# A fused attention and mixture-of-adapters kernel: quads of x copied whole in batches 0 to 6, and another order table

## The chip, the cores and the metric

One core of a Trainium2 chip runs the whole kernel in one launch. The metric is the device time of one execution in microseconds (us). TensorE (PE) does matrix products and transposes into PSUM, eight banks of 512 fp32 columns. VectorE (DVE) and ScalarE (ACT) carry PSUM to SBUF and do the element-wise work. GpSimd (POOL) issues the loads, SyncE (SP) and ScalarE's queue the stores, and 16 DMA engines move the data.

## What is computed

Squared-ReLU attention over 8 batches, 12 heads, 448 positions and head size 64, and then, on its output as 3584 rows of 768, a top-2 mixture of 8 rank-16 adapters that is added to the row:

```
scores = q @ k.T / sqrt(64)
attn   = maximum(scores, 0)**2 / 448
x      = (attn @ v), heads joined: 3584 x 768
logits = x @ w_gate                      # 3584 x 8
w      = softmax over the two largest logits of a row
out    = x + sum over those two e of  w_e * (x @ A[e]) @ B[e]
```

## The kernel before

**Units of work.** The twelve heads of a batch are worked on in three *quads* of four; 24 quads in all, numbered batch by batch. A quad in batches 0 to 6 has seven *steps* (a block of 64 keys of each of the four heads), so steps 0 to 146; batch 7 is cut in two unequal parts of the rows and has steps 147 to 173. A *tile* is 128 rows of x: 28 tiles, in groups of three, the last alone. Every piece of work is an `Op` with a name and a number:

- `tp` transposes q or k of a quad on PE into PSUM (line 313), `te` copies the result to SBUF on DVE (`qT`, lines 327 and 335).
- `qk` n is the scores of step n on PE (line 452), `relu` n the ReLU of its 128x896 into `a` on ACT or DVE (lines 472 and 474), `sq` the square of two or three steps at once on DVE (line 489), `pv` n the product with v on PE (line 520).
- `x` copies the finished quad from PSUM to `xt`, as bf16, on ACT or DVE (line 565, function `xt_copy`). A quad stands in two banks, 448 columns in each, and is copied by two ops, one for each bank; in batch 7 there are four for a quad, of 322 and 126 columns.
- `z` is a tile's x times `awg`, which holds the eight adapters' A and the gate's weights side by side (128 columns of A, then 8 of the gate; line 582, 6 matmuls); `gmax`, `gd`, `gu`, `gt`, `gsg`, `gw`, `gzp` find the two largest logits and weigh z (lines 603 to 626), `zt` transposes it (line 644), `zT` copies it out (line 661).
- `b` is half a tile of the output: three matmuls that put x itself into the bank (line 728) and the product with B (line 737, two matmul instructions in fp32). In tiles 15 to 23 x comes instead by a transposing DMA on SP (`xb`, line 677), and `b` is the product with B alone. `o` moves the half tile to `osb` (ACT or DVE, line 773; in tiles 15 to 23 an addition on DVE, line 764), and `st` stores a tile of 384 KB (line 783) through SP, in tiles 24 and 26 through ACT's queue; tile 27 goes as two halves, SP and ACT.
- Ops without a name of their own are `f` and a number: f0 to f10 are the start, f11 to f83 the loads of 224 KB for a quad (two DMAs each, line 185) with the small weights, f84 to f91 the transposes and copies of quad 0. f24 loads B (line 248), f58 is q of quad 16, f80 is k of quad 23, f87 transposes the last four key blocks of quad 0 (`k_rest`).

**What sets the order.** Nothing is planned at run time or by the compiler: the string `ORDER` lists every op; `ordered()` walks it, and `kernel` calls each op's function in that order, which makes the order on every engine's own queue. A suffix `@n` gives the first PSUM bank of an op, `:A` or `:D` the engine of an evacuation. The durations in the `op(...)` calls, `take` and `give` and `lat` are for the search that made the table and reach no instruction. SBUF buffers come from pools (`POOLS`: five for q, five for k, eight for v, eleven for `a`, four for `osb`); a load or an evacuation whose pool is full waits on its queue until the earlier user of a buffer is done, and everything behind it on that queue waits as well.

PE works either in four 64x64 quadrants (`tp`, `qk`, `pv`) or with the whole array of 128x128 (`z`, `zt`, `b`, `aw`).

Of the kernel before, what the change touches and what calls it, by code (L numbers as in the profile page):

```python
# [33 lines left out]
C = dict(late=6, xi=(), om=(), merge_x=0, sqp=((999, (2, 2, 3)),), om2=(), fl=(), gf=(), ai=4, tg=((15, 3), (18, 3), (21, 3)), sp=(), xbdur=1.45, bx=8, xh=2, apart=3, apcap=1, gl=(3, 1), tqlat=2.0)  # L34
# [5 lines left out]
f4 f3 f1 f0 f2 f6 f5 f8 f7 f11 f9 f10 f84@0 f12 f88 f85@2 f90 f89 f13 f87@4 qk0@6 f91 qk1@0 relu0:D qk2@2 f14  # L40
relu1:A qk3@4 relu2:D relu3:A tp2@6 f17 qk4@0 te2 relu4:A qk5@2 qk6@4 sq2 tp3@6 f16 relu5:A f86@0 te3 relu6:A
sq0 qk7@0 f15 qk8@2 qk9@6 relu7:A tp4@4 relu8:D relu9:A f18 qk10@0 te4 qk11@2 relu10:A qk12@6 sq4 tp5@4 f19
relu11:A qk13@0 relu12:A te5 tp6@2 f26 sq9 relu13:A qk14@4 qk15@6 tp7 relu14:A f23 sq7 pv0@0 pv1 pv2 relu15:A
pv3 qk16@4 te6 pv4 pv5 f20 relu16:A pv6 qk17@6 x13:D pv7@2 relu17:A qk18@4 sq11 f22 pv8 pv9 x12:A qk19@6
relu18:A pv10 qk20@0 relu19:D f21 pv11 relu20:A pv12 pv13 qk21@4 sq16 x27:A qk22@6 f27 qk23@0 relu21:A aw1@3
sq14 relu22:A f33 x26:D relu23:A qk24@4 tp8@6 ae1 f25 relu24:A sq18 qk25@0 qk26@2 tp9 relu25:A f55 pv14@4 pv15
pv16 te8 relu26:A pv17 qk27@0 f31 pv18 pv19 relu27:A pv20 sq23 qk28@2 qk29@6 x41:A f28 qk30@0 x40:D relu28:A
aw0@5 sq25 relu29:A f29 relu30:A qk31@2 ae0 tp10@6 tp11 f32 relu31:A sq21 qk32@4 qk33@0 relu32:A te10 pv21@2 f30
pv22 pv23 relu33:A qk34@4 sq30 qk35@6 relu34:A qk36@0 f37 relu35:D relu36:A qk37@4 pv24 pv25 relu37:A pv26 sq32
f35 qk38@6 tp12@0 pv27 relu38:A tp13 qk39@4 f43 x55:A te12 qk40@6 x54:A z0@3 relu39:A sq35 qk41@0 f34 z1  # L50
relu40:A qk42@4 relu41:D z2 relu42:A f38 qk43@6 gmax0 tp14@0 relu43:A sq28 qk44@4 tp15 f42 relu44:A gd0 qk45@6
gu0 te14 relu45:A qk46@4 f50 gt0 sq39 qk47@0 relu46:A pv28@6 pv29 pv30 gsg0 pv31 f24 relu47:A qk48@4 pv32 gw0
pv33 sq44 f48 pv34 relu48:A qk49@0 gzp0 x69:A f36 tp18@4 sq37 relu49:A tp19 pv35@2 zt0@7 zt1 zt2 x68:A f41 te18
qk50@0 zT0:A pv36 pv37 relu50:A qk51@6 sq46 pv38 pv39 f47 relu51:A pv40 qk52@4 qk53@0 pv41 relu52:A x82:D tp16@6
tp17 relu53:A te16 qk54@4 b2@2 relu54:A f44 sq49 qk55@0 o2:A qk56@6 qk57@4 relu55:A relu56:D b0@2 f49 x83:A
relu57:D qk58@0 o0:A qk59@6 f39 relu58:A z3@3 z4 sq51 relu59:A qk60@4 qk61@0 z5 f40 sq56 relu60:A b4@2 relu61:A
gmax3 qk62@6 f46 sq58 b1@4 relu62:A gu3 gd3 qk63@0 o4:A gt3 f65 sq42 qk64@6 gsg3 o1:A b3@5 relu63:A gw3 gzp3
b5@2 f51 relu64:A sq60 zt3@4 zt4 o3:A zt5 pv42@0 o5:A pv43 st2 qk65@6 zT3:A sq53 pv44 pv45 relu65:A qk66@2 st4
pv46 pv47 pv48 relu66:A tp20@4 st0 qk67@6 x96:D tp21 x97:A te20 f53 pv49@2 relu67:A pv50 qk68@0 pv51 pv52 sq63
relu68:A pv53 f66 pv54 pv55 qk69@4 qk70@6 x110:A relu69:D qk71@0 relu70:A f45 b6@2 x111:D relu71:A qk72@4 o6:D  # L60
tp22@6 relu72:A sq65 qk73@0 tp23 pv56@2 relu73:A pv57 f74 qk74@4 te22 pv58 pv59 relu74:A pv60 qk75@0 f79 pv61
sq67 pv62 relu75:A qk76@6 b8@4 f64 relu76:A x124:D qk77@0 x125:A sq70 tp24@6 relu77:A tp25 qk78@2 f59 z6@5 te24
relu78:A qk79@0 z7 relu79:A f52 o8:D qk80@2 qk81@6 sq72 z8 relu80:A b10@4 f54 gmax6 relu81:A sq77 qk82@0 tp26@2
# [81 lines left out]
def build(k=None, c=C):  # L145
# [159 lines left out]
    def tp(b, q):  # L305
# [57 lines left out]
        if b >= c["bx"]:  # L363
            return turn_qk(b, q)
# [590 lines left out]
```

## Time and profile before

| what | value |
|---|---|
| median of three runs | 181.69 us (181.57 to 182.73) |
| span of the profiled execution, first to last instruction | 179.6 us |
| time of the profiled execution itself | not listed apart; median less span is 2.09 us |
| PE, DVE, ACT busy | 165.1, 163.5, 156.2 us |
| POOL busy | 90.7 us |
| granted clock of TensorE | 1.00 all through |

A row of the timeline gives the start of a run of equal instructions, the time from its start to the end of its last one, engine, line, operation, output and inputs, count, and in brackets the idle time of the engine ahead of it and what ended it. Instructions overlap at their ends, so the *pitch* of an operation (from its start to the start of what follows it on the engine without idle time) is shorter than its duration. The chain of waits lists start, length and owner of each piece of the work that ended last.

### The profile page before, as it was taken

Reading aid. Unit: us, or ns where it says so; the run is one execution under the profiler, and the core shown is the slowest. Engines: PE = TensorE matmul, PEld = TensorE weight load, DVE = VectorE, ACT = ScalarE, POOL = GpSimd, SP = SyncE. Lnnn points to the kernel's source line nnn. Section 1 sums busy time; section 2 is a strip of 40 time slices with the busy share of each in tenths; the row PEclk is TensorE's granted clock in tenths of the full one; section 3 lists DMA queues with packets and bytes.
Section 4 is the critical chain, followed back from the end, with each engine's and each line's share of the span. In section 5 each row is a group of like instructions: output and inputs, shape, how many; then the busy total and the mean of one; then the engine's idle time right before and its main releaser. Section 6 shows DMA issues by size and latency. Waiting matters only on the chain.

```text
span 179.6 us, 7694 instructions
## 1 busy us (share of the span) xinstructions
PE 165.1 (92%) x3366; PEld 99.2 (55%) x3366; DVE 163.5 (91%) x254; ACT 156.2 (87%) x240; POOL 90.7 (50%) x155
## 2 busy tenths in 40 slices
PE   7887998888899999999979899999999999999990
PEld 2445476454535665646646465655666557576650
DVE  0699999999989999999999899999999999999831
ACT  3399999999999999999998999999999899993120
POOL 7999997988869377850966867250000000000000
PEclk9999999999999999999999999999999999999999
DMA  4999999999999999994699999988495663515644
GB/s 90 126 170 188 164 112 183 164 180 178 202 180 152 186 303 166 175 166 130 84 176 299 197 185 268 237 118 222 113 171 149 45 223 63 189 42 211 230 194 158
DMA packets 33985, 30.49 MB, mean 170 GB/s; under 512 B 11488, under 2 KB 30432, under 8 KB 33952
## 3 DMA queue, kind: packets, MB, share of 16 engines
q0 software_dynamic: 22000, 17.03, 65.7%
q1 hardware_dynamic: 11376, 11.90, 22.1%
q10 hardware_dynamic: 576, 1.08, 1.6%
q8 instruction: 26, 0.43, 0.9%
q14 instruction: 7, 0.06, 0.1%
HBM read 33.84 MB, written 11.01 MB: 250 GB/s over the span
## 4 chain that ended last, share of the span: by engine, by line
PE 44%; ACT 16%; DMA 16%; POOL 15%; issue 4%; DVE 2%; ACTq 0%; POOLq 0%
PE ps L737 17%; ACT a L472 14%; DMA q<-in_q_dram 9%; PE ps L452 9%; PE ps L520 8%; POOL k L185 5%; PE ps L582 4%; POOL v L185 4%; DMA B<-in_moe_B_dram 4%; POOL q L185 3%; PE ps L728 3%; DMA k<-in_k_dram 3%; PE ps L313 2%; ACT osb L773 2%; PE ps L644 1%
## 5 line engine op out<-in xcount | busy, mean ns | idle before, releaser
L472 ACT ACTIVATE a<-ps 128x896 bf16<-128x896 f32 (+3 forms) x158 | 132.7, 961 | 3.3 <-PE ps L452 3.0
L489 DVE TENSOR_TENSOR a<-a 128x1792 bf16<-128x1792 bf16 (+4 forms) x75 | 88.5, 1193 | 0.0
L452 PE MATMUL ps<-qT 64*64 64x448 bf16 (+2 forms) x756 | 57.9, 345 | 4.5 <-ACT a L472 3.3
L737 PE MATMUL ps<-B,zT 128*128 128x384 f32 x112 | 47.5, 514 | 0.3 <-DMA B<-in_moe_B_dram 0.3
L520 PE MATMUL ps<-a,v 64*64 64x448 bf16 (+2 forms) x756 | 44.3, 330 | 0.8 <-ACT a L472 0.4
L452 PEld LDWEIGHTS <-qT 64*64 64x64 bf16 x756 | 25.3, 106 | 31.9 <-issue 22.9
L185 POOL DMA_DIRECT2D k<-in_k_dram x46 | 27.8, 629 | 16.3 <-PE ps L452 7.1
L185 POOL DMA_DIRECT2D v<-in_v_dram x48 | 28.8, 621 | 8.1 <-PE ps L452 3.8
L185 POOL DMA_DIRECT2D q<-in_q_dram x48 | 29.4, 639 | 3.5 <-DMA v<-in_v_dram 1.5
L520 PEld LDWEIGHTS <-v 64*64 64x64 bf16 x756 | 22.6, 106 | 7.9 <-issue 2.7
L327 DVE COPY qT<-ps 128x1792 bf16<-128x1792 bf16 x21 | 22.8, 1084 | 0.7 <-ACT a L472 0.4
L565 ACT CAST xt<-ps 128x448 bf16<-128x448 f32 (+2 forms) x37 | 19.4, 560 | 2.6 <-PE ps L520 2.3
L773 ACT COPY osb<-ps 128x384 f32<-128x384 f32 x26 | 13.1, 529 | 7.4 <-PE ps L737 5.6
L737 PEld LDWEIGHTS ps<-B,zT 128*128 128x128 f32 x112 | 17.3, 190 | 3.7 <-DMA B<-in_moe_B_dram 0.4
L474 DVE TENSOR_SCALAR a<-ps 128x896 bf16<-128x896 f32 (+1 forms) x16 | 16.9, 1069 | 0.9 <-PE ps L452 0.9
L313 PEld LDWEIGHTS <-q 64*64 64x64 bf16 x672 | 10.4, 112 | 6.9 <-issue 3.3
L582 PEld LDWEIGHTS <-xt 128*128 128x128 bf16 x168 | 10.5, 98 | 5.7 <-issue 4.7
L582 PE MATMUL ps<-awg,xt 128*128 128x136 bf16 x168 | 13.5, 223 | 0.0
L728 PEld LDWEIGHTS <-xt 128*128 128x128 bf16 x114 | 8.0, 98 | 9.9 <-issue 8.1
L313 PE MATMUL ps<-identb,q 64*64 64x64 bf16 x672 | 10.9, 197 | 2.3 <-DMA q<-in_q_dram 1.1
L728 PE MATMUL ps<-identb,xt 128*128 128x128 bf16 x114 | 12.7, 220 | 0.2
L565 DVE CAST xt<-ps 128x448 bf16<-128x448 f32 (+2 forms) x17 | 9.6, 570 | 0.2 <-PE ps L520 0.2
(47 smaller groups left out, 97.9 us busy)
## 6 DMA issues: line engine op xcount, KB each, us to landing
out_dram<-osb SPq DMA_DIRECT2D x25, 384.0 KB, 4.2
q<-in_q_dram POOLq DMA_DIRECT2D x48, 112.0 KB, 5.0
v<-in_v_dram POOLq DMA_DIRECT2D x48, 112.0 KB, 4.9
k<-in_k_dram POOLq DMA_DIRECT2D x46, 112.0 KB, 4.9
out_dram<-osb ACTq DMA_DIRECT2D x2, 384.0 KB, 2.3
B<-in_moe_B_dram POOLq DMA_DIRECT2D x1, 384.0 KB, 6.6
xb<-xt SPq DMA_TRANSPOSE x18, 3.2
a_raw<-in_moe_A_dram POOLq DMA_DIRECT2D x1, 192.0 KB, 5.4
```

The costliest lines, as they stand in the source:

```text
L185: nc.gpsimd.dma_start(out=t[g * PH : g * PH + PH], in_=k.qkv[w][b, g, :, 2 * q : 2 * q + 2, :])
L313: nc.tensor.transpose(k.ps_b[sl * PH : sl * PH + PH, o.banks[g], (w * J + j) * PH : (w * J + j) * PH + PH], source(w, j)[r, sl], k.identb[ ...
L327: nc.vector.tensor_copy(t.rearrange("p g w x -> p g (w x)"), k.ps_b[:, m.banks[0] : m.banks[0] + 2, : 2 * S])
L452: nc.tensor.matmul(out=bank(o, sl)[g * PH : g * PH + PH, at : at + w].rearrange("k (j p) -> k j p", j=J), lhsT=t[r, g, 1, j * PH : j * PH ...
L472: nc.scalar.activation(out, flat(qk_ops[n], w), ACTF.Relu, scale=k.relu_scale)
L474: nc.vector.tensor_scalar(out, flat(qk_ops[n], w), k.relu_scale, 0.0, op0=ALU.mult, op1=ALU.max)
L489: nc.vector.tensor_mul(a, a, a)
L520: nc.tensor.matmul(out=bank(head, g)[sl * PH : sl * PH + PH, :w], lhsT=vn[r, sl, j * PH : j * PH + PH], rhs=T["a", g0][r, x + sl * width(n ...
L565: evac(w, lambda cp, g=g: cp(k.xt[:, g * QUADS + q, b * S + x0 : b * S + x1].rearrange("d (p j) -> d p j", j=J), bank(src, g)[:, :w].rearr ...
L582: nc.tensor.matmul(out=bank(zops[0])[:, t * ZW : t * ZW + ZW], lhsT=k.xt[:, do, 128 * tiles[t] : 128 * tiles[t] + 128], rhs=k.awg[:, do, : ...
L728: nc.tensor.matmul(out=out(h)[:, x * 128 : x * 128 + 128], lhsT=k.xt[:, 3 * h + x, c0 : c0 + 128], rhs=k.identb, start=(x == 0), stop=Fals ...
L737: nc.tensor.matmul(out=o, lhsT=T["zT", g0][:, zi], rhs=rhs, start=xb is not None, stop=True, skip_group_check=True,)
```

## The change

1. `merge_x` lists the quads of batches 0 to 6, and `xt_copy` copies each of these in one op of 128x896 from both banks: 21 ops in the place of 42. Batch 7 keeps its two ops for each part.
2. `ORDER` is another table of the same ops (without the 21). The counts by engine, before and after: `relu` 158 ACT and 16 DVE, then 157 and 17; `x` 37 and 17, then 25 and 8 (of batches 0 to 6: 28 and 14 of 448 columns, then 17 and 4 of 896); `o` 26 and 12, then 23 and 15; `zT` 6 and 4, then 7 and 3. The rest is the same.
3. `awg` holds each adapter's 16 columns and its gate column together (8 times 17), so `gmax` and `gu` read the logits at a stride of 17, and `gzp` reads 16 of 17.
4. Code that no setting used goes (`turn_qk`, `idle`, `xi`, `z64`), groups of four tiles become possible and aren't used, and the search's durations and keys change.

```
-C = dict(late=6, xi=(), om=(), merge_x=0, sqp=((999, (2, 2, 3)),), om2=(), fl=(), gf=(), ai=4, tg=((15, 3), (18, 3), (21, 3)), ...
+C = dict(late=6, sq=((999, (2, 2, 3)),), merge_x=tuple((b,0,q) for b in range(7) for q in range(3)), two=(), groups=(3, 3, 3, 3, 3, 3, 3, 3, 3, 1), ai=4, tg=((15, 3), (18, 3), (21, 3)))
...
-        if n < c["merge_x"]:
+        if (b, u, q) in c["merge_x"]:
             return [
                 evac(2 * w, lambda cp: cp(k.xt[:, q::QUADS, b * S + x0 : b * S + x1].rearrange("d g (p j) -> d g p j", j=J),
                                        pair(src)[:, :, :w].rearrange("d g (j p) -> d g p j", j=J)),
...
-                    for rhs, lo, hi in ((k.a_raw[:, :, i, :], 0, RE), (k.g_raw[:, i, :], RE, ZW)):
+                    for rhs, lo, hi in ((k.a_raw[:, :, i, :], 0, R), (k.g_raw[:, i, :, None], R, R + 1)):
...
-                nc.vector.max(mx[:, t, :], z3()[:, t, RE:ZW])
+                nc.vector.max(mx[:, t, :], zv()[:, t // m, t % m, :, R])
```

The table's beginning, the first loads of the middle that the text speaks of, and the end:

```
-f4 f3 f1 f0 f2 f6 f5 f8 f7 f11 f9 f10 f84@0 f12 f88 f85@2 f90 f89 f13 f87@4 qk0@6 f91 qk1@0 relu0:D qk2@2 f14
-relu1:A qk3@4 relu2:D relu3:A tp2@6 f17 qk4@0 te2 relu4:A qk5@2 qk6@4 sq2 tp3@6 f16 relu5:A f86@0 te3 relu6:A
+f0 f4 f6 f8 f1 f3 f7 f2 f9 f10 f84@0 f5 f85@2 f88 f90 f11 f89 qk0@2 f87@0 qk1@4 f91 relu0:A relu1:A qk2@6 relu2:D f12
+f13 qk3@0 tp2@2 f14 qk4@4 relu3:A qk5@6 relu4:A tp3@0 relu5:A f15 qk6@4 te2 sq0 te3 f17 relu6:A f16 qk7@0 tp4@6 sq2
...
-x139:A qk88@6 qk89@2 o9:A zT6:D qk90@0 relu88:A relu89:D st8 tp28@4 tp29 relu90:A f80 qk91@6 te28 pv70@2 pv71
-relu91:A pv72 pv73 qk92@0 sq84 f60 pv74 pv75 relu92:A pv76 qk93@4 b14@6 x153:D x152:A f58 relu93:A sq81 qk94@0
+sq72 st4 f80 pv66 qk86@2 o9:A relu85:A pv67 qk87@0 pv68 pv69 relu86:A sq79 f60 zt6@6 relu87:D zt7 x138:A zt8 qk88@2
+tp26@0 tp27 qk89@4 zT6:A sq77 relu88:A te26 relu89:A b14@6 o14:A qk90@2 pv70@0 pv71 tp28@4 tp29 qk91@6 sq81 relu90:A
+te28 pv72 sq88 relu91:A qk92@2 pv73 pv74 pv75 pv76 tp30@4 pv77@6 tp31 relu92:A qk93@2 f58 pv78 pv79 st8 x152:A
...
-z27@0 b52@1 o43 gmax27 st42 gd27 gu27 b53@3 gt27 o52:A gsg27 b50@2 gw27 gzp27 o53:D zt27@4 b51@5 st53 o50:A
-b48@3 o51:D zT27:A st50 b49@2 o48:D b54@3 o49:A st49 b55@2 o54:D st54 o55:D st55
+st42 o50:A b53@7 zt27@6 st44 st46 zT27:A o53:D o52:A b51@3 o51:D st53 b54@6 b48@7 b55@3 b49@2 st50 o54:D o55:A st54
+st55 o48:D o49:A st49
```

In the loads ahead of f80 on POOL, the table before has f74, f79 and f64 (k of quad 21, q of quads 23 and 18); the table after has none of these there. B (f24) is POOL's 31st op behind quad 0's in the table before and its 28th in the table after. Stores and transposes on SP are in another order, too.

## Rows read from the trace of the kernel before

**Rows 1.** Page: busy time of each engine, share of the span, instructions.
```profile
PE 165.1 (92%) x3366; PEld 99.2 (55%) x3366; DVE 163.5 (91%) x254; ACT 156.2 (87%) x240; POOL 90.7 (50%) x155
```

**Rows 2.** Windows: us, PE, PEld, DVE, ACT, POOL busy, clock, DMA share, GB/s.
```profile
105.00:120.00 15.00, 14.96 (x295) 9.15 (x292) 14.64 (x23) 14.86 (x23) 8.45 (x15) 1.00 1.09 212
120.00:140.00 20.00, 19.90 (x474) 12.69 (x466) 19.52 (x27) 19.86 (x32) 0.00 (x0) 1.00 0.77 157
```

**Rows 3.** Timeline of ACT, 71 to 76 us.
```profile
71.23 0.61 ACT L565 CAST xt<-ps 128x448 bf16<-128x448 f32 x1
71.64 4.26 ACT L472 ACTIVATE a<-ps 128x896 bf16<-128x896 f32 x5
75.63 0.64 ACT L773 COPY osb<-ps 128x384 f32<-128x384 f32 x1
```

**Rows 4.** Timeline of DVE, 65 to 72 us.
```profile
65.28 1.09 DVE L474 TENSOR_SCALAR a<-ps 128x896 bf16<-128x896 f32 x1
66.28 0.61 DVE L565 CAST xt<-ps 128x448 bf16<-128x448 f32 x1
...
70.86 0.61 DVE L565 CAST xt<-ps 128x448 bf16<-128x448 f32 x1
71.39 1.08 DVE L489 TENSOR_TENSOR a<-a 128x1792 bf16<-128x1792 bf16 x1
```

**Rows 5.** Groups by line and shape: busy us, mean ns, idle time before.
```profile
L472 ACT ACTIVATE a<-ps 128x896 bf16<-128x896 f32 x132 | 114.7, 1001 | 2.2 <-PE ps L452 1.9
L565 ACT CAST xt<-ps 128x448 bf16<-128x448 f32 x28 | 16.5, 625 | 0.0
L565 DVE CAST xt<-ps 128x448 bf16<-128x448 f32 x14 | 8.6, 617 | 0.2 <-PE ps L520 0.2
```

**Rows 6.** Timelines of PE and ACT, the first 9 us.
```profile
6.81 1.73 PE L452 MATMUL ps<-qT 64*64 64x448 bf16 x16
...
5.91 0.53 ACT L335 COPY qT<-ps 128x448 bf16<-128x448 bf16 x1 [2.90 <-PE ps L313]
7.83 1.73 ACT L472 ACTIVATE a<-ps 128x896 bf16<-128x896 f32 x2 [1.38 <-PE ps L452]
```

**Rows 7.** Chain of waits, then timeline of ACT, around 50 us.
```profile
44.23 6.55 DMA B<-in_moe_B_dram
...
51.78 0.48 ACT L773 COPY osb<-ps 128x384 f32<-128x384 f32 x1 [0.31 <-PE ps L737]
```

**Rows 8.** Timelines of POOL, PE and ACT, 85 to 96 us.
```profile
85.61 1.20 POOL L185 DMA_DIRECT2D k<-in_k_dram  x2 [6.06 <-PE ps L452]
...
93.87 0.41 PE L313 MATMUL ps<-identb,q 64*64 64x64 bf16 x26 [0.91 <-DMA q<-in_q_dram]
...
94.51 0.92 ACT L472 ACTIVATE a<-ps 128x896 bf16<-128x896 f32 x1 [0.52 <-PE ps L452]
```

**Rows 9.** Timeline of PE, 108 to 111 us.
```profile
108.57 0.86 PE L737 MATMUL ps<-B,zT 128*128 128x384 f32 x2
109.27 0.33 PE L728 MATMUL ps<-identb,xt 128*128 128x128 bf16 x3
109.44 0.86 PE L737 MATMUL ps<-B,zT 128*128 128x384 f32 x2
110.23 0.76 PE L452 MATMUL ps<-qT 64*64 64x448 bf16 x12
```

**Rows 10.** Timeline of PE, the last scores and the last outputs.
```profile
159.79 0.45 PE L452 MATMUL ps<-qT 64*64 64x126 bf16 x20
160.89 2.82 PE L737 MATMUL ps<-B,zT 128*128 128x384 f32 x8
174.39 0.86 PE L737 MATMUL ps<-B,zT 128*128 128x384 f32 x2
```

**Rows 11.** DMA issues: size, count, median us from issue to landing.
```profile
out_dram<-osb ACTq DMA_DIRECT2D x2, 384.0 KB, 2.3
...
out_dram<-osb ACTq DMA_DIRECT2D x1, 192.0 KB, 1.9
```

More of the change, by code (lines that the diff above doesn't have):

```diff
@@ L17 @@
 SPIN = 8
+APART = 3
 PH = 64
+GM = 4
 QUADS = 3
@@ L186, in fn @@
                                     in_=k.qkv[w][b, g, :, 2 * q : 2 * q + 2, :])
-        o = op(("POOL",), 1.17, fn, deps=deps, kind="load", take=(nm, "lane"), give=("lane",))
+        o = op(("POOL",), 1.17, fn, deps=deps, kind="load", take=((nm, (b, q)),))
         o.mb = 1.35
@@ L537, in pv @@
         return o
-    def idle(n, head, after):
-        def fn():
-            for g in range(2):
-                r = slice(g * PH, g * PH + PH)
-                for sl in range(2):
-                    nc.tensor.matmul(
-                        bank(head, g)[sl * PH : sl * PH + PH, :S], lhsT=k.zeros[r, :PH], rhs=k.zeros[r, :S],
-                        start=False, stop=False,
-                    )
-        return op(PE, S / 2400 + 0.01, fn, after=after, mode="64", kind="spin", ni=8, key=("fl", n))
     def xt_copy(n):
@@ L638, in gate @@
+        o_sg = op(ACT, 0.12, f_sig, deps=[o_t], key=("gsg", g0))
+        o_w = op(DVE, 0.1, f_w, deps=[o_sg], key=("gw", g0))
+        o_zp = op(DVE, dve(n * RE), f_zp, deps=[o_w], free=[(zops[0], None)], give=(("w", g0),), key=("gzp", g0))
         zts = []
@@ L698, in outputs @@
         evs, obs, prev = [], {}, None
-        xi = None
-        if tl in c["xi"]:
-            def f_xi():
-                for do in range(DO):
-                    for i in range(2):
-                        r = slice(i * PH, i * PH + PH)
-                        for j in range(2):
-                            nc.tensor.matmul(
-                                out=bank(xi, i)[j * PH : j * PH + PH, do * PH : do * PH + PH],
-                                lhsT=k.xt[r, do, c0 + j * PH : c0 + j * PH + PH], rhs=k.identb[r, r],
-                                start=(do == 0), stop=False, skip_group_check=True,
-                            )
-            xi = op(PE, 0.17, f_xi, mode="64", kind="xi", deps=xdeps[tl], banks=("o", 2), take=("osb",), ni=8 * DO,
-                    key=("xi", tl))
-        merged = xi is not None and tl in c["om"]
-        two = tl in c["om2"]
+        two = tl in c["two"]
         def osb():
@@ L721, in osb, with out @@
             return T["osb", tl]
+        def out(h):
+            return bank(obs[0], h) if two else bank(obs[h])
         for h in range(2):
-            xb = xb_of.get((tl, h)) if xi is None else None
+            xb = xb_of.get((tl, h))
             def f_b(h=h, xb=xb):
-                for x in range(0 if xb or xi else 3):
+                for x in range(0 if xb else 3):
                     nc.tensor.matmul(
@@ L748, in outputs @@
                 last = zuse[g0] == 0
-            give = ("zT",) if last else ()
-            prev = op(PE, 0.645 if xb or xi else 0.81, f_b, mode="128", kind="b",
-                      deps=[o_zT, b_load] + ([] if xb else [xi] if xi else xdeps[tl]), after=prev,
-                      banks=None if xi or two and h else ("o", 1 + two), take=() if h or xi else ("osb",), give=give, key=("b", 2 * tl + h), ni=4 if xb or xi else 10)
+            prev = op(PE, 0.68 if xb else 0.868, f_b, mode="128", kind="b",
+                      deps=[o_zT, b_load] + ([] if xb else xdeps[tl]), after=prev,
+                      banks=None if two and h else ("o", 1 + two), take=() if h else (("osb", tl),),
+                      give=(("zT", g0),) if last else (), key=("b", 2 * tl + h), ni=4 if xb else 10)
             obs[h] = prev
```

325 lines of the change are left out of this document (110 added, 215 removed).

## The prediction

> **What bounds the kernel now.** I read the busy times first. PE, DVE and ACT are each busy for more than 156 us of the span of 179.6 [rows 1], so no one engine is the bound by its total. The windows then show where the three press on each other: from 105 to 140 us, PE, DVE and ACT are each busy for at least 97% of the time [rows 2]. In this stretch, work that goes from ACT and DVE alone shortens nothing unless PE has less to do as well, and the reverse. [...]
>
> Outside that stretch the timelines show four places where the engines don't press on each other. At the start ACT has no work until 7.83 us, and its first ReLU waits for the scores [rows 6]. Near 51 us ACT waits for an output product, and the chain behind it runs through the load of B, which took 6.55 us from its issue at 44.23 [rows 7]. Near 93 us PE is idle for 0.91 us for a quad's q, and ACT for 0.52 us after it [rows 8]; the cause stands in the same group: POOL sat idle for 6.06 us before a load of k, and the late load of q is the second one behind it. That k is f80, of quad 23, which nobody needs before step 157; it waits for one of five k buffers, of which two hold the k of quads 18 and 21, loaded early as well. The fourth place is the end: the last scores begin at 159.79 us, and PE then works alone to 175.25 [rows 10], while ACT runs out of work.
>
> **The sum.** It is made against the profiled execution, whose span is 179.6 us. Its own time is not listed; I put the 2.09 us by which the median stands above the span on top of both sides, so the terms apply to 181.69.
>
> *Copies and engines.* Pitches count here, since instructions of one engine overlap. On ACT a copy of 448 columns takes 71.64 - 71.23 = 0.41 us and a ReLU of 896 takes (75.63 - 71.64)/5 = 0.80 [rows 3]. On DVE they take 71.39 - 70.86 = 0.53 and 66.28 - 65.28 = 1.00 [rows 4]. The trace has no copy of 896; the ReLU of that shape is the nearest row on both engines. Before: 28 x 0.41 + 14 x 0.53 = 18.9 us. After: 17 x 0.80 + 4 x 1.00 = 17.6. That is 1.3 less, about 0.06 for each quad: nearly all of a copy's time is its columns, and those stay. One ReLU more on DVE costs 0.20, and three outputs more on DVE cost 3 x 0.12, taking the step between the two 448 copies. Net -0.75 over two engines that are both full, so -0.35 each. Ends: 0 where PE sets the pace, -0.75 if one engine gets it all. The new stride of the gate's reads moves as many elements in as many instructions; I take 0. It lies on DVE between the squares, and if that cover were missing, ten groups at a few hundredths would be some 0.3.
>
> *Start.* The table puts qk0 before f87, so the first scores no longer stand behind the transposes of `k_rest`. These began at 6.3 us and the scores at 6.81 [rows 6]; the scores can now begin when ACT's copy of q ends, 5.91 + 0.53 = 6.44. ACT also gets relu0 and relu1, where it had its first ReLU at 7.83; DVE's first one comes later in exchange, as relu2. ACT gains up to 0.9, DVE loses some of it. I take -0.3; ends 0 and -0.9.
>
> *Load of B.* It is three POOL operations earlier in the table, and the q loads ahead of it find their buffers free earlier. Three operations of 1.2 us are more than ACT's gap of 0.31 [rows 7]. I take -0.3; ends 0 and -0.6, twice the gap, as DVE waits at the same place.
>
> *Load of q for quad 16.* In the new table f80 is still early, but of the far-ahead loads of k and q before it none is left, so a k buffer is free when POOL comes to it. The wait of 0.91 on PE, and the 0.52 of ACT that lies inside its shadow, go [rows 8]. Next late would be k of quad 16, which has to wait until quad 13 is transposed, some 17 steps before its own use. I take -0.8; ends 0, and -1.4 for both gaps in a row.
>
> *PE's changes between quadrants and whole array.* Counted in the tables: 100 before, 108 after, six of the eight in the last 75 steps. From b to b the pitch of the pair is 109.27 - 108.57 = 0.70, and from b to qk it is 110.23 - 109.44 = 0.79 [rows 9], so a change costs 0.09. Eight cost 0.7. Where ACT and DVE hold PE up it is hidden. I take +0.4; ends 0 and +0.8.
>
> *Work left for PE after the last scores.* Before, 15 `b` are listed behind qk173, 7 of them of the short form; after, 13 with 5 short. Two short ones are 2 x 2.82/4 = 1.4 us [rows 10]. They are done earlier instead, where PE is nearly full [rows 2], so I count half: -0.7; ends 0 and -1.4.
>
> *Last store.* The table now ends with tile 24, a whole tile through ACT's queue, instead of half of tile 27: 2.3 us to landing against 1.9 [rows 11], +0.4; ends 0 and +0.4.
>
> Sum: -0.35 - 0.3 - 0.3 - 0.8 + 0.4 - 0.7 + 0.4 = -1.65, so 180.0. All far ends the one way give 176.6, the other way 182.9.
>
> [...]
>
> **The rivals.**
>
> *A: each merged copy saves a fixed part.* If what counts is an instruction's length and not its pitch, because a lone copy between waits has nothing to overlap with, 28 x 0.625 + 14 x 0.617 = 26.1 us become 17 x 1.001 + 4 x 1.09 = 21.4 [rows 4, 5]: 2.35 on each engine in place of 0.65, so 178.3. Against it: in the rows read, ACT goes from copy to ReLU without a gap [rows 3].
>
> *B: the table closes every gap.* Start, B, q and the end at their far ends, the rest as taken: -0.35 - 0.9 - 0.6 - 1.4 + 0.4 - 1.4 + 0.4 = -3.85, so 177.8. For it: two of the gaps come from loads and are not work. Against it: from 105 to 140 us there is little left to close [rows 2].
>
> *C: the gaps move.* Loads of another order wait elsewhere, the stretch with three full engines gives nothing back, and only copies, changes of mode and the last store count: -0.35 + 0.4 + 0.4, so 182.1. Or, as near, the copies are all that differs.
>
> *D: the merged copy stands in PE's way (slower).* Two copies could run side by side or free their banks one after the other, 0.41 us apart; a merged one holds both for 0.80. In 11 of the 21 quads the new table lets the very next PE operation that takes one of these banks follow with no ReLU listed between, and PE's queue is in order: all scores and transposes behind it wait too. At 0.80 - 0.41 = 0.39 each [rows 3] that is 4.3 us, less 1.65: 184.3. It decides where PE arrives at the bank before the copy has ended; with four such places or fewer the time stays under that of before. Against it: PE usually stands a step ahead of ACT, so ACT still has a ReLU to do meanwhile.
>
> **How the numbers follow.** A measurement of this kernel tells about 1%, 1.8 us, from no change. The forecast has 0.45, with a range of its own from 179.2 to 181.0; as 180.0 lies close to the bound of 179.9, I put 0.18 of it below and 0.27 within 1%. A has 0.13, B 0.14, C 0.13, D 0.15. Faster by over 1%: 0.18 + 0.13 + 0.14 = 0.45. Within 1%: 0.27 + 0.13 = 0.40. Slower: 0.15. For the range, 177.8 takes in A and half of B; 183.2 takes in C, the end of the known costs at 182.9, and D with some seven of its eleven places.
>
> **What would show it.** In the profile after: a first ReLU on ACT before 7.4 us; no idle time of PE for q after 80 us, and no POOL wait of several us ahead of a k; 128x896 casts at a mean of about 1.0 us and a pitch near 0.80 (A wants one clearly under that, or gaps around the old copies); PE ending less than 15.4 us after the last scores begin. D would show as PE idle, released by ACT or DVE at line 565. The prediction is wrong if ACT and DVE together have less idle time by far more than 2 us between 10 and 160 us, or if SP's stores hold up an output because its `osb` buffer is not free.

## The result, and the profile after

The kernel after takes 182.68 us (median of 20 runs, 181.50 to 185.12) where the one before takes 181.6 beside it: a ratio of 1.0075 with an interval of 1.0054 to 1.0096. A second set of runs gave 1.0081 [1.0045, 1.0116]. The medians differ by 1.08 and 1.25 us and the ratios make 1.4 and 1.5, as they leave out the few slow executions of either kernel. So the change costs some 0.8%, about 1.3 us, where I had forecast a gain of 1.65. 182.68 lies inside the range of 177.8 to 183.2, but on the other side of no change.

The profiled execution of after is its fastest run (181.50 with a span of 179.5), so its rows show where time moved, but not the whole loss. The busy times, which answer to [rows 1]:

```profile
PE 165.2 (92%) x3366; PEld 97.1 (54%) x3366; DVE 162.5 (91%) x248; ACT 156.6 (87%) x225; POOL 90.6 (50%) x155
```

The windows of after, columns as in [rows 2]:

```profile
10.00:20.00 10.00, 7.60 (x228) 3.92 (x223) 10.00 (x12) 9.90 (x13) 9.69 (x15) 1.00 1.29 178
80.00:100.00 20.00, 19.75 (x450) 11.64 (x450) 19.90 (x27) 20.00 (x29) 13.04 (x22) 1.00 0.93 169
...
105.00:120.00 15.00, 15.00 (x343) 9.05 (x346) 14.50 (x22) 14.99 (x24) 8.32 (x15) 1.00 1.10 175
120.00:140.00 20.00, 20.00 (x437) 11.77 (x429) 19.90 (x29) 19.55 (x29) 0.00 (x0) 1.00 0.56 161
140.00:160.00 20.00, 20.00 (x349) 12.21 (x345) 19.68 (x42) 17.47 (x29) 0.00 (x0) 1.00 0.48 131
```

And windows of before that [rows 2] does not have, the last of them from the second profile of that kernel (before_again, below):

```profile
10.00:20.00 10.00, 8.12 (x244) 4.70 (x237) 10.00 (x13) 10.00 (x13) 9.46 (x16) 1.00 1.21 181
80.00:100.00 20.00, 18.71 (x408) 11.05 (x398) 19.42 (x25) 19.13 (x30) 10.70 (x18) 1.00 0.89 173
140.00:160.00 20.00, 19.99 (x382) 12.34 (x378) 19.79 (x42) 18.60 (x35) 0.00 (x0) 1.00 0.44 124
...
80.00:100.00 20.00, 19.17 (x403) 11.13 (x399) 19.32 (x26) 19.59 (x31) 10.49 (x18) 1.00 0.88 173
```

Read PE's column, the second number. From 105 us on PE is busy in every window of after, 55.00 of 55.00 us, and it was at 54.85 before: there is nothing to win there from an engine other than PE. From 80 to 100 us PE has 1.04 us less idle time, of which the wait for q was 0.91; against the second profile of before, where that wait was 0.45, it is 0.58 less. From 10 to 20 us PE has 0.52 more in this profile. That figure is not stable: over the first 20 us PE is idle for 4.47 us in after and for 3.66 in after_again, which has the same start (there at a mean granted clock of 0.83); before has 3.76.

The same at the start, in the groups by line (busy and mean, then idle time of PE before the group and what ended most of it), of before and of after:

```profile
L452 PE MATMUL ps<-qT 64*64 64x448 bf16 (+2 forms) x756 | 57.9, 345 | 4.5 <-ACT a L472 3.3 <-DVE qT L335 0.6 <-DVE a L474 0.2
```
```profile
L387 PE MATMUL ps<-qT 64*64 64x448 bf16 (+2 forms) x756 | 61.1, 346 | 6.1 <-ACT a L407 3.4 <-DVE qT L333 1.4 <-DVE qT L325 0.8
```

PE waits for DVE's copies of q and k for 1.4 + 0.8 = 2.2 us; the row of before lists 0.6. The first ReLU on ACT does come earlier, as I said it would, and the copies have the predicted length and pitch. But what ACT gains in the first 10 us, 0.67 us of busy time, DVE loses, 0.88: its only ReLU there is relu2, where it had relu0 and relu2. The windows, before and after, then the timeline of ACT in after, and the groups of the merged copy:

```profile
0.00:10.00 10.00, 8.12 (x120) 3.72 (x121) 4.44 (x11) 4.05 (x6) 8.88 (x20) 1.00 0.78 112
```
```profile
0.00:10.00 10.00, 7.93 (x118) 3.91 (x118) 3.56 (x9) 4.72 (x7) 8.89 (x20) 1.00 0.80 113
```
```profile
7.14 2.54 ACT L407 ACTIVATE a<-ps 128x896 bf16<-128x896 f32 x3 [0.68 <-PE ps L387]
...
45.97 1.06 ACT L466 CAST xt<-ps 128x896 bf16<-128x896 f32 x1
46.77 1.08 ACT L407 ACTIVATE a<-ps 128x896 bf16<-128x896 f32 x1
```
```profile
L466 ACT CAST xt<-ps 128x896 bf16<-128x896 f32 x17 | 16.8, 988 | 0.0
L466 DVE CAST xt<-ps 128x896 bf16<-128x896 f32 x4 | 4.4, 1088 | 0.3 <-PE ps L442 0.3
```

46.77 - 45.97 = 0.80, the pitch taken from [rows 3]. The new stride of the gate's reads costs nothing that counts: by their groups on DVE, `gmax` takes 162 ns where it took 159, `gu` 177 where it took 174, and `gzp` 552 in both.

One of my signs did not come: POOL still waits for several us ahead of a k (timeline of POOL in after). It is k of quad 16, the one I had called next late, and PE has no wait for it.

```profile
82.02 1.19 POOL L183 DMA_DIRECT2D k<-in_k_dram  x2 [5.59 <-PE ps L387]
```

The last scores and the last output on PE, which answer to [rows 10]:

```profile
159.93 0.56 PE L387 MATMUL ps<-qT 64*64 64x126 bf16 x28
...
173.42 0.86 PE L618 MATMUL ps<-B,zT 128*128 128x384 f32 x2
```

PE ends 14.35 us after the last scores begin, where it was 15.46: less work is left, as forecast. But the last scores begin no earlier, so the pieces that were done in advance have, as it seems, only changed places; no run shows their price there apart.

Three things are new in after. One is a stall of PE inside a product with v, ended by "issue", so by nothing that the profile shows (timeline of PE):

```profile
67.88 0.92 PE L442 MATMUL ps<-a,v 64*64 64x448 bf16 x13
69.13 0.38 PE L442 MATMUL ps<-a,v 64*64 64x448 bf16 x3 [0.34 <-issue]
```

The second is the end. From the last evacuation's end to the end of the span it takes 179.5 - 174.88 = 4.6 us, where the trace of before has 179.6 - 175.85 = 3.75 (timeline of ACT, then the piece of the chain of waits that ends the first row's wait):

```profile
173.45 0.48 ACT L645 COPY osb<-ps 128x384 f32<-128x384 f32 x1 [2.68 <-DMA out_dram<-osb]
...
174.40 0.48 ACT L645 COPY osb<-ps 128x384 f32<-128x384 f32 x1 [0.47 <-PE ps L618]
```
```profile
171.28 2.19 DMA out_dram<-osb
```

The third stands in the first of these rows: an output waits 2.68 us for a store to free its `osb` buffer, and one on DVE waits 0.8. Neither profile of before has such a wait, and I had named it as a sign that the prediction is wrong. In this profile it costs little, as PE is busy without a break from 160 us to its end at 174.28, and the last copy starts 0.12 us later.

### The profile page after: what moved, and what is told of

The parts are those of the page before. It is cut to its first block, busy times and chain, and to the rows that moved or that the text cites. A ratio compares the mean times of both kernels' runs of the same rounds, so it can differ in the third digit from the quotient of the medians.

```text
span 179.5 us, 7676 instructions
## 1 busy us (share of the span) xinstructions
PE 165.2 (92%) x3366; PEld 97.1 (54%) x3366; DVE 162.5 (91%) x248; ACT 156.6 (87%) x225; POOL 90.6 (50%) x155
## 3 DMA queue, kind: packets, MB, share of 16 engines
q10 hardware_dynamic: 576, 1.08, 1.6%
## 4 chain that ended last, share of the span: by engine, by line
PE 56%; DVE 22%; ACT 8%; issue 5%; DMA 5%; POOL 2%; ACTq 0%; DVEq 0%; POOLq 0%
PE ps L618 16%; PE ps L387 13%; PE ps L442 13%; DVE a L424 10%; ACT a L407 6%; PE ps L489 5%; DVE qT L325 4%; DVE a L409 3%; PE ps L613 3%; PE ps L311 3%; DMA out_dram<-osb 3%; DMA q<-in_q_dram 2%; DVE qT L333 1%; PE ps L553 1%; POOL q L183 1%
## 5 line engine op out<-in xcount | busy, mean ns | idle before, releaser
L387 PE MATMUL ps<-qT 64*64 64x448 bf16 (+2 forms) x756 | 61.1, 346 | 6.1 <-ACT a L407 3.4
L442 PE MATMUL ps<-a,v 64*64 64x448 bf16 (+2 forms) x756 | 44.9, 330 | 1.1 <-ACT a L407 0.4
L387 PEld LDWEIGHTS <-qT 64*64 64x64 bf16 x756 | 24.8, 105 | 37.2 <-issue 29.1
L618 PEld LDWEIGHTS ps<-B,zT 128*128 128x128 f32 x112 | 17.3, 190 | 3.0 <-issue 0.4
L409 DVE TENSOR_SCALAR a<-ps 128x896 bf16<-128x896 f32 x17 | 18.4, 1085 | 0.3 <-PE ps L387 0.3
L466 ACT CAST xt<-ps 128x896 bf16<-128x896 f32 x17 | 16.8, 988 | 0.0
L645 ACT COPY osb<-ps 128x384 f32<-128x384 f32 x23 | 12.2, 531 | 3.2 <-DMA out_dram<-osb 2.7
L489 PEld LDWEIGHTS <-xt 128*128 128x128 bf16 x168 | 10.6, 98 | 4.7 <-issue 4.1
L613 PEld LDWEIGHTS <-xt 128*128 128x128 bf16 x114 | 7.4, 97 | 9.1 <-issue 8.2
L311 PE MATMUL ps<-identb,k 64*64 64x64 bf16 x644 | 10.0, 196 | 0.0
```

Source lines behind the costliest of these rows:

```text
L311: nc.tensor.transpose(k.ps_b[sl * PH : sl * PH + PH, o.banks[g], (w * J + j) * PH : (w * J + j) * PH + PH], source(w, j)[r, sl], k.identb[ ...
L387: nc.tensor.matmul(out=bank(o, sl)[g * PH : g * PH + PH, at : at + w].rearrange("k (j p) -> k j p", j=J), lhsT=t[r, g, 1, j * PH : j * PH ...
L409: nc.vector.tensor_scalar(out, flat(qk_ops[n], w), k.relu_scale, 0.0, op0=ALU.mult, op1=ALU.max)
L442: nc.tensor.matmul(out=bank(head, g)[sl * PH : sl * PH + PH, :w], lhsT=vn[r, sl, j * PH : j * PH + PH], rhs=T["a", g0][r, x + sl * width(n ...
L466: evac(2 * w, lambda cp: cp(k.xt[:, q::QUADS, b * S + x0 : b * S + x1].rearrange("d g (p j) -> d g p j", j=J), pair(src)[:, :, :w].rearran ...
L489: nc.tensor.matmul(out=bank(zops[0], t // m)[:, t % m * ZW : t % m * ZW + ZW], lhsT=k.xt[:, do, 128 * tiles[t] : 128 * tiles[t] + 128], rh ...
```

## The experiments

Where a kernel was timed in several rounds, its ratio is to the kernel before, on the same chip.

### Are the merged copies the cause?

after_again is the kernel after once more (1.0081, above). The end takes 4.60 us again, but PE ends at 176.03 us, 1.75 later than in the first profile, with waits of 0.67 and 1.12 us ended by "issue". So the first profile was a lucky execution. The first experiment undoes the merging in the new table, the second does it alone in the old one.

```
after_two_copies:
-merge_x=tuple((b,0,q) for b in range(7) for q in range(3))
+merge_x=()
-... x26:A ...            (and the other 20)
+... x26:A x27:A ...
before_one_copy:
-merge_x=0
+merge_x=147
-... x13:D ... x12:A ...  (and the other 20)
+... x12:A ...
```

> The changed kernel once more, for a second profile beside the first, whose span (179.5 us) is as short as that of before although the median time is 1.08 us longer. Expected ratio to before 1.0075 by every theory. Theory END (the last store, a whole tile on ACT's queue, gives back what PE gains): again some 4.6 us from the last evacuation to the end of the span, against 3.75 before, and PE ending about 1 us earlier than before. Theory MIDDLE (loads or buffers that now and then arrive late, so that the first profile was a lucky execution): PE's end lies 1 us or more later than the first profile's 174.3 us, with idle time on PE that the first profile does not have.

> The new table with each merged x copy taken apart again into two copies of 448 columns, one behind the other on the same engine. COPIES HARM (rival D: the merged copy holds both banks): the time falls, ratio 1.002 or less. COPIES HELP as the pitches say (0.04 to 0.07 us each, some 0.6 us on each engine): the time rises, ratio about 1.011. COPIES DON'T MATTER: 1.0075, as the changed kernel.

> The old table with the two x copies of each quad of batches 0 to 6 made one, where the first of the two stood, 14 on ACT and 7 on DVE (half of the 28 and 14). COPIES HELP as the pitches say: ratio 0.996. By the lengths of the instructions (rival A): 0.987. COPIES HARM: over 1.005, up to 1.013. If it is within 0.2% of 1, the merging is no part of the loss.

after_two_copies took 182.56 us, 1.0065 [1.0032, 1.0098]: the same as after. In the new table the merging neither gains nor costs anything that shows. (Two copies side by side on both engines were not run in it.) before_one_copy took 186.07, 1.0279 [1.0229, 1.0328]: 5 us slower. Timelines of ACT and PE in it:

```profile
66.72 0.91 ACT L556 CAST xt<-ps 128x896 bf16<-128x896 f32 x1
...
67.68 0.33 PE L724 MATMUL ps<-identb,xt 128*128 128x128 bf16 x3 [0.44 <-ACT xt L556]
```

PE stands for 0.44 us until the copy ends, and such waits recur (24, 31, 40, 125, 153 us). PE's waits for the copies of line 556 come to 3.3 us, where the profile of before lists none. So the mechanism of my rival D is real in a table that was not made for it. It is not shown to be all of the 5 us: in 14 of the 21 quads the old table has the two copies on different engines, and the edit takes that away as well. In the new table D does not occur: no profile of it lists a wait of PE for the merged copies.

### The end, and the early matmuls for the clock

The new table also moved f86, eight matmuls on zeros that nobody reads, from behind relu5 to behind relu26, and in several of its profiles the granted clock falls for some microseconds in the first 20 us (after_again: a mean of 0.83 over these 20 us). So the end and f86 were put back, alone and together, and f86 was moved alone in the old table.

```
after_other_end:
-b54@6 b48@7 b55@3 b49@2 st50 o54:D o55:A st54 st55 o48:D o49:A st49
+b48@7 b49@2 b54@6 b55@3 st50 o48:D o49:A st49 o54:D st54 o55:A st55
after_spin_back:
-te2 sq0 ... relu26:A f86@6 qk28@6
+te2 f86@2 sq0 ... relu26:A qk28@6
before_spin_late:
-relu5:A f86@0 te3 ... te8 relu26:A
+relu5:A te3 ... te8 f86@0 relu26:A
```

> The new table, but the last twelve entries in an order like the old one's: b48, b49, b54, b55, then tile 24's outputs and store, then tile 27's, whose two half stores are the last. END: the 0.85 us behind the last evacuation go, ratio about 1.003. Else the ratio stays at 1.0075 and the loss lies ahead of the end.

> The new table with one entry moved: f86, eight matmuls on zeros that nobody reads, from behind relu26 back to behind te2, near relu5 as in the old table. CLOCK (without f86 there, PE's granted clock falls to 0.5 between 9 and 15 us in most executions, and what PE falls behind is not made up): granted clock 1.00 in the profile until the last evacuation, ratio about 1.004 in the place of 1.0078. NO CLOCK (DVE and ACT set the pace there, so PE's slow stretch costs nothing): ratio 1.0075 or, by f86's own 0.4 us, 1.009.

> f86 back and tile 27 last, both. If CLOCK and END hold and add up: 1.0078 - 0.0035 - 0.003, so about 1.001. If only END holds: 1.005.

> The old table with f86 moved the other way, from behind relu5 to just ahead of relu26. CLOCK: granted clock falls to 0.5 near 10 us in the profile, ratio 1.003 to 1.006. NO CLOCK: ratio 0.998 to 1.000, as f86 now runs where PE has time.

> The old kernel once more, for a second profile: does its clock stay at 1.00 and does PE stand still anywhere between 60 and 75 us with nothing released, as in three profiles of the new table (0.34, 1.12 and 1.43 us)? CLOCK: no fall near 10 us or a short one. If the clock falls as long as in the new table, f86 is not the cause. Ratio 1.000.

after_other_end: 182.08, 1.0051 [1.0017, 1.0086], and 1.0055 [1.0019, 1.0090] in a later set. after_spin_back: 182.86, 1.0077 [1.0041, 1.0114]. Both edits: 182.08, 1.0046 [1.0009, 1.0084]. before_spin_late: 181.54, 1.0034 [0.9995, 1.0072]. before_again, the old kernel once more: 1.0000 [0.9956, 1.0044]; its profile has a granted clock of 1.00 up to 160 us and no wait of PE on "issue".

The end costs 0.3% in both pairs, 0.5 us, by the differences 1.0081 - 1.0051 and 1.0077 - 1.0046; the intervals overlap, so its size is not sure. The profiles make it smaller. From the end of the last ReLU to the end of the span it is 17.3 us in all six profiles of the old table with its copies as they were, 16.9 to 17.0 with the new end and 16.7 to 16.8 with the old end put back: the store wins 0.45 us, and PE, which then waits for an `osb` buffer, ends 0.3 later. So the end of after as a whole is shorter than before by 0.35 us, and the loss lies ahead of it.

f86 shows no clear effect: putting it back gains nothing, though it did not keep the clock up either (a mean of 0.91 from 10 to 30 us in the profile of after_spin_back). before_spin_late, whose profile has a granted clock of 0.68 from 10 to 20 us, lies where the theory of the clock had it, with an interval that takes in 1. The clock carries little of the loss. The profile of after_other_end has 1.00 all through, and that execution took 182.63, above the median of its kernel. Twelve executions of after, after_again and after_two_copies have a mean granted clock of 0.99 or more; their median is 182.4, still some 0.9 us above before. Over 87 executions of the new table in seven runs, 0.01 less of mean clock goes with 0.21 us more time. The new table's mean is 0.983 and the old one's 0.992, so some 0.2 us of the loss may be the clock's (an estimate).

### The stall near 70 us

In every profile of the new table, the same instruction is late, the 14th of 16 matmuls of one product with v: by 0.34 us in after, 1.12 in after_again, 1.43 in after_other_end, and 0.29 to 1.18 in the six others whose code before it is as long. Timeline of PE in after_other_end, and its DMA view from 66 to 72 us (queue, packets, MB, share of 16 engines):

```profile
68.39 0.92 PE L442 MATMUL ps<-a,v 64*64 64x448 bf16 x13
70.73 0.38 PE L442 MATMUL ps<-a,v 64*64 64x448 bf16 x3 [1.43 <-issue]
```
```profile
q0 software_dynamic: 1121, 0.89, 98.5%
q1 hardware_dynamic: 151, 0.39, 17.9%
q8 instruction: 1, 0.02, 1.0%
```

One packet of code lands in this time (it starts at 68.50 us), on DMA engines that loads fill. The page counts 26 such packets in an execution, 0.43 MB and so 16 KB in each, and PE has 3366 matmuls with as many weight loads: 259 of these to a packet, so I took a piece for 256 of them (an estimate). To see whether code is what PE waits for, I moved the places at which one piece ends and the next begins, by half a piece and by a whole one.

```
 def spin():          # f86
     for _ in range(2):
         ...
+    for _ in range(16):            # after_shift_whole: 32
+        for g in range(2):
+            for sl in range(2):
+                nc.tensor.matmul(bank(sp, g)[sl * PH : sl * PH + PH, :8], lhsT=k.zeros[g * PH : g * PH + PH, :PH],
+                                 rhs=k.zeros[g * PH : g * PH + PH, :8], start=True, stop=True)
```

> The new table with tile 27 last, and 64 matmuls of 8 columns more in f86 (28 us, a stretch in which PE waits for its inputs anyway). With its weight loads that is 128 more instructions of PE ahead of everything later, so that the places at which PE's code is fetched move by half a piece. Nothing else near 70 us is changed. Theory (PE stands still behind the 13th matmul of a pv near 70 us because its next instructions are fetched late, past full DMA engines): the stall of 1.43 us with nothing released (after_other_end) goes from this pv, and a shorter one or none shows elsewhere between 55 and 80 us; without a new one the time falls by about 0.7 us, less up to 0.5 us for the matmuls added: ratio to before about 1.002 in place of 1.005. Rival (a wait that the profile does not show, for a bank or for v): the stall stays behind the same 13th matmul with 0.3 to 1.5 us, ratio 1.005 or more.

> As the run before, but with 128 small matmuls, so 256 more instructions of PE: if a piece holds 256 of them (16 KB), the places of the fetches stand where they stood. Theory of late instructions: the stall is back behind the same 13th matmul near 70 us, with 0.3 to 1.5 us, ratio 1.005 to 1.008 with the added matmuls. Rival that more instructions anywhere shift the timing and so remove the stall: none there, ratio as in the run before or better.

Timeline of PE at the same product, first with half a piece:

```profile
70.14 0.94 PE L447 MATMUL ps<-a,v 64*64 64x448 bf16 x16
70.89 0.37 PE L392 MATMUL ps<-qT 64*64 64x448 bf16 x4
```

and with a whole one, and that kernel's waits of PE (in total, times, longest):

```profile
72.75 0.92 PE L447 MATMUL ps<-a,v 64*64 64x448 bf16 x13
74.52 0.38 PE L447 MATMUL ps<-a,v 64*64 64x448 bf16 x3 [0.85 <-issue]
```
```profile
PE ps L311 <- issue: 2.3, 2, 1.2
...
PE ps L351 <- issue: 1.4, 1, 1.4
...
PE ps L447 <- issue: 0.9, 1, 0.9
```

With half a piece the stall is gone, and the 16 matmuls run in one go. With a whole one it is back behind the 13th, and the code packet has moved with it, to 72.32 us. At this product PE goes on 2.2 to 2.4 us after that packet starts, in all ten profiles of the new table that have the stall. In the two profiles of before, the packet of the piece with the same number starts 2.8 and 3.1 us ahead of its first matmul, and PE doesn't wait.

The places say the same. The stall stands behind 1374 matmuls of PE, or 1502 with the whole shift. Every other wait of PE on "issue" of over 0.3 us, in any profile, stands behind 606, 734, 862, 990 or 2270 matmuls. Each of these numbers is 94 and a multiple of 128, and 128 matmuls with their weight loads are 256 instructions. So PE waits for code. That the loads delay the packet is what the 98.5% suggests; no run shows it.

A late piece costs its full time. From 60 to 80 us after_other_end has 1.09 us more of the stall than after, and PE, DVE and ACT are each busy for 1.07 to 1.10 less (windows of after, then of after_other_end):

```profile
60.00:80.00 20.00, 19.41 (x386) 10.53 (x385) 19.48 (x27) 19.48 (x28) 12.09 (x21) 1.00 1.14 207
```
```profile
60.00:80.00 20.00, 18.34 (x368) 10.01 (x360) 18.39 (x26) 18.38 (x26) 12.45 (x21) 1.00 1.13 199
```

Seven profiles of the new table (after, after_again, after_two_copies, after_other_end and its repeat, after_spin_back, after_spin_back_other_end) have 0.3 to 1.8 us of waits on "issue", 1.0 in the mean; six of the old one have 0 to 0.3, 0.1 in the mean.

The times went otherwise than expected: 185.64 (1.0204 [1.0127, 1.0281]) and 186.15 (1.0212 [1.0144, 1.0280]) for 1.002 and some 1.006. The whole shift has three further stalls on code of 1.1 to 1.4 us before 50 us, as its waits show. The half one has two others, PE at 47.10 us for 1.46 and at 155.31 for 1.28. The second is for a buffer of `osb`. The first is put down to a ReLU of ACT that had ended at 46.19, but it stands behind 990 matmuls and ends 2.4 us after a packet of code starts, so it is code as well:

```profile
47.10 0.38 PE L392 MATMUL ps<-qT 64*64 64x448 bf16 x4 [1.46 <-ACT a L412]
```

### Are PE's changes of mode paid in full?

One kernel has 14 changes fewer, by moving a `b` or `z` up to the one ahead of it at seven places; another has 16 more and moves nothing.

```
after_fewer_changes (on after_other_end), three of seven places:
-b10@0 qk84@2 o10:A b9@1                 +b10@0 b9@1 qk84@2 o10:A
-b15@4 relu98:A qk101@2 z9@5 ... z10     +b15@4 z9@5 z10 relu98:A qk101@2
-z15@3 z16 ... qk140@0 z17               +z15@3 z16 z17 ... qk140@0
after_more_changes (on after_other_end), in the product of a gate:
+                if tiles[t] in (10, 13, 16, 18, 19, 20, 21, 23):
+                    for sl in range(2):
+                        nc.tensor.matmul(bank(zops[0], t // m)[sl * PH : sl * PH + PH, 496:504], lhsT=k.zeros[:PH, :PH],
+                                         rhs=k.zeros[:PH, :8], start=True, stop=True)
                 for do in range(DO):
```

> The new table with tile 27 last and 14 changes of PE fewer between quadrants and whole array (95 in the place of 109), made at seven places between steps 84 and 140 by moving a b or a z up to the one ahead of it, past one or two qk. Theory (from 100 us on PE never waits in the new table, so what PE has to do is the time): 14 x 0.09 to 0.12 = 1.3 to 1.6 us come off the end, 180.6 where after_other_end had 182.08, ratio to before 0.995 to 0.998. Rival (ACT and DVE hold PE up there as well, and a change is hidden beside them, as I had half assumed with +0.4 for eight): nothing, ratio 1.005. Or the moved pieces come too early for their inputs: slower, with PE waiting for zT or xt between 80 and 140 us.

> The new table with tile 27 last, and ahead of the gate products of eight tiles (10, 13, 16, 18, 19, 20, 21, 23), which each follow other work of the whole array, two matmuls of 8 columns in 64x64 quadrants: 16 changes more between quadrants and whole array, with the order as it was. The eight lie behind 95 us, where PE never waits in the new table. Theory (a change is paid in full there): 16 x 0.09 to 0.12 = 1.4 to 1.9 us, with at most 0.4 for the 16 small matmuls: about 183.9 where the kernel without them has 182.1, PE's last matmul later by as much. Rival (PE has slack there that the profile shows as busy time): 0 to 0.4 us, 182.3.

> The kernel that the run before is to be compared with, on the same chip: 182.1, ratio to before 1.005, the stall behind the 13th matmul of the pv near 70 us again between 0.3 and 1.5 us.

after_fewer_changes took 184.71, 1.0165 [1.0122, 1.0209]: slower by 1.1% than without the edit (by the ratios, as the two ran on different chips). The last sentence of its expectation holds: the order now lets PE arrive too early elsewhere (timeline of PE):

```profile
92.58 0.57 PE L387 MATMUL ps<-qT 64*64 64x448 bf16 x8 [0.89 <-DVE a L409]
...
107.75 0.41 PE L311 MATMUL ps<-identb,q 64*64 64x64 bf16 x28 [0.89 <-DVE a L409]
```

It says nothing of a change's price. after_more_changes took 183.39, 1.0111 [1.0067, 1.0154], beside 182.43, 1.0055 [1.0019, 1.0090], without them: 0.96 us for eight pairs, half of the 1.4 to 1.9 expected; the two intervals overlap. Timeline of PE with a pair, and at the same place without:

```profile
139.93 0.28 PE L557 MATMUL ps<-identf,zp 128*128 128x128 f32 x1
140.14 0.19 PE L490 MATMUL ps<-zeros 64*64 64x8 bf16 x2
140.27 0.53 PE L493 MATMUL ps<-awg,xt 128*128 128x136 bf16 x6
140.63 0.28 PE L557 MATMUL ps<-identf,zp 128*128 128x128 f32 x1
```
```profile
140.33 0.28 PE L553 MATMUL ps<-identf,zp 128*128 128x128 f32 x1
140.44 0.52 PE L489 MATMUL ps<-awg,xt 128*128 128x136 bf16 x6
140.80 0.28 PE L553 MATMUL ps<-identf,zp 128*128 128x128 f32 x1
```

From `zt` to `zt` it is 0.70 us in place of 0.47: 0.23 for two changes with two small matmuls, so at most 0.115 for one. By the times it is 0.06 for one; by [rows 9] it was 0.09. The eight changes of the new table cost it 0.5 to 0.9 us. These rows show a cost; what PE does in that time is in no row.

### The two load terms, alone

```
before_q16_first, before_q16_again (on the old table):
-relu90:A f80 qk91@6 ... x152:A f58 relu93:A
+relu90:A qk91@6 ... x152:A f58 f80 relu93:A
before_q16_B: the same, and
-relu42:A f38 qk43@6 ... pv31 f24 relu47:A
+relu42:A f24 f38 qk43@6 ... pv31 relu47:A
```

> The old table with one load moved: k of quad 23 (f80) stands behind q of quad 16 (f58) on POOL in the place of ahead of it. By the term for the load of q in the prediction, PE's wait of 0.91 us and what hangs on it go: between 80 and 100 us PE loses 1.0 us less, 180.7, ratio to before 0.994 to 0.996. Rival (the gap moves: k of quad 17 or 18 comes late in turn, behind f80's wait for a k buffer): PE idle for q or k between 95 and 115 us, ratio 1.000.

> The old table with k of quad 23 behind q of quad 16, once more: 181.0, ratio 0.9964 again if the gain was real (under 0.9985), 1.000 if it was the spread of the runs; PE without a wait of over 0.3 us for q behind 80 us.

> The same, and the load of B three POOL operations earlier, as far as the new table has it. By the terms of the prediction: -0.8 and -0.3, 180.4, ratio 0.994, and PE has no wait for B near 51 us. Rival (the load that stands in B's old place comes later in turn, and ACT's queue is held by PE there anyway): as the run before, 0.9964.

before_q16_first: 181.0, 0.9964 [0.9929, 0.9998]; again: 181.18, 0.9986 [0.9955, 1.0017]. Timeline of POOL and the window of the first:

```profile
84.48 1.18 POOL L182 DMA_DIRECT2D q<-in_q_dram  x2 [0.50 <-PE ps L310]
85.64 1.20 POOL L182 DMA_DIRECT2D k<-in_k_dram  x2
```
```profile
80.00:100.00 20.00, 19.65 (x415) 11.57 (x413) 19.99 (x25) 19.92 (x31) 12.15 (x21) 1.00 1.02 189
```

The load of q is issued at 84.48, where it was 87.94 in the profile of before, PE's wait for it is gone, and PE has 0.94 us less idle time there (0.48 less than in the second profile of before). The gain in time, 0.25 and 0.65 us in the two sets, has the right sign, but the second set doesn't tell it from none. It is the fastest version found, by a margin that two sets leave unsure. before_q16_B: 1.0000 [0.9952, 1.0047]: the load of B moved up brings nothing that shows, though an interval of 0.9 us each way could hide the 0.3 of the forecast. PE has no wait for B near 51 us, but before_again has none either. A load of k that B passed is late in turn (timeline of PE):

```profile
46.85 0.41 PE L310 MATMUL ps<-identb,k 64*64 64x64 bf16 x26 [0.56 <-DMA k<-in_k_dram]
```

## Why the prediction was wrong

The steps of the sum, with what was found of each:

| step | forecast, us | found, us |
|---|---|---|
| copies and engines | -0.35 | 0 (after_two_copies) |
| start | -0.3 | about 0: ACT +0.67 busy, DVE -0.88 (profile of after) |
| load of B | -0.3 | 0, not sure to 0.9 (before_q16_B) |
| load of q for quad 16 | -0.8 | -0.25 and -0.65 (the old table with that alone) |
| changes of mode | +0.4 | +0.5 to +0.9 (after_more_changes) |
| work left after the last scores | -0.7 | -1.1 there, as much ahead of it, so 0 (profile of after, argued) |
| last store | +0.4 | +0.85 in the profile; the old end wins back 0.2 (profiles) to 0.5 (times) |
| late code on PE | not in the sum | +0.9 in the mean (profiles; shown by the shifts) |
| clock | not in the sum | about +0.2 (an estimate) |

Two steps failed. One is a term that the sum did not have: PE waits for its own code, 0.9 us more in the mean than before. The profile of before has no such wait of 0.2 us or more; its piece for the same place came in time, by half a microsecond.

The other step stands behind two of the terms: I credited a gain to ACT, or to an earlier place in the order, in stretches where PE was full already. "Copies and engines" gave half of 0.75 us to the end, and "work left for PE after the last scores" half of 1.4, although [rows 2] had PE at 14.96 of 15.00 and 19.90 of 20.00. The prediction's own first part said that work which goes from ACT and DVE alone shortens nothing there; the sum then counted half of it. The first was worth nothing (after_two_copies). Of the second, PE did have 1.1 us less to do after the last scores, and the end is shorter by 0.35 us with the longer store; but in the seven profiles named above the last ReLU ends at 162.5 to 164.8 us, where it was 161.4 to 162.9 before (163.6 with f86 moved).

"Start" failed on what is late next. I followed ACT, which got its ReLU 0.69 us earlier, and not DVE, which stood idle longer and whose copies of q and k PE then waited for.

"Load of B" failed in its bound: the wait is gone in after, but it was not in every execution before, and what B passes on POOL's queue comes later itself.

"Load of q" was right in mechanism: PE's idle time went, by 0.9 to 1.0 us against the first profile of before and by 0.5 to 0.6 against the second, and the time fell by 0.25 and 0.65. The sum took one execution's wait for every execution's. "Changes of mode" and "last store" had the right sign and were low.

Of the rivals, C, "the gaps move", at 182.1, was nearest: it counted the changes and the last store and gave back the rest. That it came so near is in part luck, as it had no late code either. D described a real mechanism that shows only in the old table (before_one_copy: PE stands for 0.44 us at 67 us until the copy ends). A's fixed part did not show: the merged copy's pitch is 0.80 us for 896 columns, where the old one's is 0.41 for 448 [rows 3].

The found terms, with 0.2 to 0.85 for the store, add up to between +1.15 and +2.6; the measured +1.3 is at the lower end. The start, the work left and the mean of late code come from profiles of single executions, and no run takes the late code alone away, so the exact balance stays open. From 40 to 60 us PE was busy for 18.51 us in after and 17.80 in after_again, against 17.98 in the profile of before: whether the new table gains there can't be told from these.

## What to carry to other kernels

Before crediting a saved instruction or an earlier place, read in the windows whether the engine that sets the pace in that stretch has idle time at all. Where it has none, only its own work counts, and only if the order isn't disturbed; where it has some, ask of each gap what will be late next on the queue that you rearrange. When an order is made for one set of instructions, test the instruction change and the order apart: the same merging was worth 0 in one table and came with 5 us of loss in the other. Where an order or the length of the code changes, look for waits on "issue" and count at which instruction they stand.

## What the hardware showed that I had not expected

PE's code comes in pieces, and a piece can be late in straight code: 0.29 to 1.43 us for one near 70 us, 0.35 to 1.46 us for others once the pieces lay elsewhere. The size of a piece fits 256 instructions: 256 more brought the stall back to its place, 128 took it away. Most pieces came in time: of some 26 pieces in an execution, PE stood for none or one in the old table and for four at most, in the two shifted kernels. Where PE stood for over 0.3 us, it went on 2.2 to 3.0 us after the packet of the piece had started.

Adding 64 or 128 matmuls of 8 columns at 28 us, where PE had idle time, made the kernel slower by 1.5%; the profiles show three further stalls on code with 128, and with 64 one of 1.46 us beside the wait for `osb`.
